# Fused attention and two MoE layers on one core: float32 attention for the first 256 tokens, weight loads eight pieces ahead

## The chip, the cores and the metric

One NeuronCore of a Trainium2 chip runs the whole program in one launch. Its engines are TensorE (PE in the profile, its weight loads PEld), VectorE (DVE), ScalarE (ACT), GpSimd (POOL) and SyncE (SP), which issues nearly all of the DMAs. The metric is the device time of one execution in microseconds, the median over runs.

## The reference

q, k and v are 4 batches x 8 heads x 576 tokens x 64 in float32. Attention is causal by blocks of 64; its output, 2304 tokens of 512, goes through a dense layer with an ELU, and that through a second layer with a skip test and one of eight experts for each token:

```python
scores = scale * np.matmul(q, k.transpose(0, 1, 3, 2))
mask = block_i >= block_j                       # blocks of 64 tokens
attn = np.exp(scores - np.max(scores, axis=-1, keepdims=True))
attn = attn / (np.sum(attn, axis=-1, keepdims=True) + 1e-09)
x = np.matmul(attn, v)                          # -> 2304 x 512
h = x @ w_in                                    # 512 x 2048, float64 weights
g = np.where(h > 0.0, h, np.exp(np.minimum(h, 0.0)) - 1.0)
x = g @ w_out                                   # 2048 x 512
# second layer: x @ w_skip > 0 picks the tokens, argmax(x @ w_gate) the expert,
# out = x + gate * (relu(x @ w1[e]) @ w2[e]) for the picked tokens
```

## The kernel before, in words

**Order.** Every operation is first recorded, not issued (the helper `record`, L306, whose line 320 is the line of nearly all rows in the trace). `order` (L159) then places all of them, engine by engine, by a table of costs (`cost`, L323), by priorities (`rc.base`, where -300 puts the start first) and by the time from which an operation may run (`rc.ready`). Each engine executes its list in that fixed order. A list can therefore stand still behind a row that waits, SP's list of DMAs too.

**Attention** is done for tiles of 128 queries (numbered n = 0 to 4 in a batch) and pairs of heads (p = 0 to 3). `prep_k` (L693), `prep_q` (L706) and `prep_v` (L725) load 128 rows of float32 and split them into a high and a low float16 half: the high half on ScalarE, the low one on VectorE. k and q are then transposed, by a DMA from SP ("kt<-k", "qt<-qq"), or for the first two tiles of batch 0 (`early`, L675) on TensorE through `turn` (L679), whose results ScalarE ("qt<-tp") or VectorE ("kt<-tp") copies out of PSUM. v is scaled by its largest square sum, which `vflat` (L621), `vmax` (L626) and `vscale` (L636) find; vflat loads all of a batch's v, 1152 KB. `s_unit` (L739) makes the scores with two float16 products and a mask ("s<-late"). `x_unit` (L761) takes the row maximum on VectorE ("mx<-s") and the exponential on ScalarE ("e<-s,mx", followed by a read of the accumulated sum). `h_unit` (L792) normalises into the high half ("ehl<-e,su", ScalarE), `l_unit` (L828) makes the low half (VectorE) and transposes the probabilities to et, by DMA or, for the early tiles, by `turn`. `pv` (L848) multiplies by v in three float16 products into PSUM ("xps") and ScalarE copies the result into xt, the input of the first layer.

**First layer.** The tokens go in nine chunks c of 256. w_in and w_out are float64, so each comes as 16 pieces of 512 KB (`raw_load`, L470), and VectorE makes float32 of a piece by one TENSOR_SCALAR and two SCALAR_TENSOR_TENSOR on its integers (`conv`, L495): "twi" for w_in, "two" for w_out. `load_to` (L1292) and `conv_step` (L1296) decide how many pieces are loaded ahead of the conversion. Chunks 0 and 1 multiply in float32: `l1` (L883) makes 256 columns of h for one of eight hidden blocks f (two pieces of w_in each, 8 matmuls of 128x256 per block shown as "h<-xt,twi x8", each recorded in two), `l1a` and `l1b` the ELU, `l2` (L928) the second product ("y<-two,g", eight rows of the trace a block). c0 does all of l1 and then all of l2; its l2 block f needs w_out pieces 2f and 2f+1. Later chunks use float16 halves of the weights, for which ScalarE sums squares ("sq<-twi", "junk<-two") to find a scale. `post` (L948) and `logits` (L986) carry a finished chunk to the second layer.

c0 holds the tokens of tiles 0 and 1 of batch 0; c1 those of tiles 2 and 3, the units i = 4 to 7 of group G1 (a unit is one head of a tile; tile 4 follows). So c1's l1 needs all four head pairs of these.

The driver (L1321 to 1428) begins with the start sequence, which the change rewrites; after it `conv_step` and the further loads are hung on points of the unit list.

Of the kernel before, what the change touches and what calls it, by code (L numbers as in the profile page):

```python
# [9 lines left out]
F32 = mybir.dt.float32  # L10
F16 = mybir.dt.float16
# [345 lines left out]
@with_exitstack  # L357
def tile_kernel(ctx, tc, q, k, v, w_in, w_out, w_skip, w_gate, w1, w2, out):
    nc = tc.nc
# [266 lines left out]
    def vmax(b):  # L626
# [4 lines left out]
        rc.scalar.activation(out=t, in_=t, func=AF.Square, accum_out=col[:, s + b:s + b + 1])  # L631
        if b == 0:

            rc.ready[len(rc.steps) - 1] = 11.5

# [43 lines left out]
    def turn(out, ins, tag, dve=False):  # L679

        t = ps.tile([128, len(ins), 128], F16, tag=tag, bufs=2, name="tp")
        for x, a in enumerate(ins):
            if isinstance(a, tuple):
                for h in range(2):
                    rc.tensor.transpose(out=t[64 * h:64 * h + 64, x, :], in_=a[h], identity=ident16)
            else:
                rc.tensor.transpose(out=t[:, x, :], in_=a, identity=ident16)
        if dve:
            rc.vector.tensor_copy(out, t)
        else:  # L690
            rc.scalar.activation(out=out, in_=t, func=AF.Copy)

    def prep_k(b, n):  # L693
# [6 lines left out]
        rc.vector.scalar_tensor_tensor(out=k1[0:r, :, 1, :], in0=raw[0:r], scalar=0.25, in1=k1[0:r, :, 0, :], op0=ALU.mult, op1=ALU.subtract)  # L700
        if early(b, n):
            turn(KT[b][:, :, n * 128:n * 128 + r], [k1[0:r, h].rearrange("p a d -> p (a d)") for h in range(H)], "y", True)
            return
        rc.sync.dma_start_transpose(out=KT[b][:, :, n * 128:n * 128 + r], in_=k1[0:r].rearrange("p h a d -> p (h a d)"))

    def prep_q(b, n):  # L706
# [7 lines left out]
        rc.vector.scalar_tensor_tensor(out=qq[0:r, 0, :, 1, :], in0=raw[0:r], scalar=0.5, in1=qq[0:r, 0, :, 0, :], op0=ALU.mult, op1=ALU.subtract)  # L714
        if early(b, n):
            turn(t[:, 0], [qq[:, 0, h].rearrange("p a d -> p (a d)") for h in range(H)], "h")
            turn(t[:, 1], [(qq[:, 0, h, 1], qq[:, 0, h, 0]) for h in range(H)], "h")
            QT[b, n] = t
            return
        rc.sync.dma_start_transpose(out=t[:, 0], in_=qq[0:r, 0].rearrange("p h a d -> p (h a d)"))  # L720
# [18 lines left out]
    def s_unit(b, p, i):  # L739
        n = i // 2  # L740
        w = 128 * (n + 1) if n < 4 else S
        parts = [(0, w)] if w <= 512 else [(0, 512), (512, w)]
        qt, kt = QT[b, n], KT[b]
        mx = sm.tile([128, 4], F32, tag="mx", bufs=4, name="mx")
        tl = []
        for m, (a, e_) in enumerate(parts):
            t = ps.tile([128, e_ - a], F32, tag="s", bufs=3, name="s")
            rc.atom()
            for ps_ in range(2):
                if n < 4:  # L750
# [41 lines left out]
    def h_unit(b, p, i):  # L792
# [6 lines left out]
        if n == 1:  # L799
            rc.vector.tensor_tensor(out=su[:, 0:1], in0=su[:, 0:1], in1=su[:, 2:3], op=ALU.add)  # L800
        rc.vector.tensor_scalar(out=su[:, 4:4 + n], in0=su[:, 0:n], scalar1=1e-9, scalar2=2.0 ** -14, op0=ALU.add, op1=ALU.mult)
        rc.vector.reciprocal(out=su[:, 6:6 + n], in_=su[:, 4:4 + n])
        nu[0] += 1
        if b == 0 and i in G[0][0]:

            pool, tag, bufs = mo, "g", GB
        elif HL.get(("wo", 7)) is not None and nu[0] % 3 == 0:
            pool, tag, bufs = wp, "wo7", 1
# [19 lines left out]
    def l_unit(b, p, i):  # L828
# [10 lines left out]
        n, nk = hl.shape[1:3]  # L839
        y = (4, 2)[x] if b == 0 and x < 2 and p % 2 else x  # L840
        et = ET[b, p, x] = ap.tile([128, n, 2 * nk, 128], F16, tag=f"et{y}", bufs=ET_BUFS[y], name="et")
        if b == 0 and i in G[0][0]:
            hf = hl.rearrange("p u n a c -> p (u n a) c")
            turn(et.rearrange("p u n c -> p (u n) c"), [hf[:, y] for y in range(2 * n * nk)], "h", p % 2 == 1)
            return
        rc.sync.dma_start_transpose(out=et.rearrange("p u n c -> p (u n) c"), in_=hl.rearrange("p u n a c -> p (u n a c)"))

    def pv(b, p, g):  # L848
# [16 lines left out]
        while t0 < t1:  # L865
# [4 lines left out]
            if c < 2:  # L870
                rc.scalar.activation(out=xt(c)[:, p, t0 - c * CT:e_ - c * CT], in_=src, func=AF.Copy, scale=st["x0"])
            else:
# [474 lines left out]
    for x in range(6):
# [633 lines left out]
```

## Time and profile before

| what | us |
|---|---|
| three runs | 726.5, 728.25, 731.14; median 728.25 |
| execution that the profile shows | 724.39 |
| its span | 722.6 |
| busy in the span: TensorE, weight loads, VectorE, ScalarE, GpSimd | 671.3, 462.8, 576.3, 514.2, 78.4 |

A stage table gives an engine's busy time in a stretch; a timeline gives one engine's rows in order, with the idle time before a group and what ended it in square brackets. [...] c0's first product begins at 47.54 us, c1's at 129.33.

### The profile page before, as it was taken

What the parts mean: (1) busy time and instruction counts of PE and PEld (TensorE: products, weight loads), DVE (VectorE), ACT (ScalarE), POOL (GpSimd) and SP (SyncE); (2) the same over time, 40 slices, a digit from 0 to 9 for tenths busy, and PEclk for the clock granted to TensorE, in tenths of its full rate; (3) what the DMA queues carried; (4) which work ended last, traced back from release to release, by engine and by line L of the source; (5) the groups of instructions that cost most, each with busy time, mean ns of one, the idle gap of its engine ahead of it and who ended that gap; (6) DMA issues with size and microseconds to landing.
All of it is one profiled execution on the core that took longest, in us unless ns stands there. A gap on an engine that the chain in (4) does not pass through costs nothing. (4 is left out here: it accounts for less than half of the span.)

```text
span 722.6 us, 17731 instructions
## 1 busy us (share of the span) xinstructions
PE 671.3 (93%) x6665; PEld 462.8 (64%) x6665; DVE 576.3 (80%) x1664; ACT 514.2 (71%) x1090; POOL 78.4 (11%) x119
## 2 busy tenths in 40 slices
PE   4679988999999999989999999999999999999994
PEld 3457643875466666647657667667576667777783
DVE  5897999988999999888969945999778654774653
ACT  5977746999986888678758745766366466887782
POOL 2000000001000100100100000000105033423112
PEclk9559999999999999999999999999999999999998
DMA  8699999895796999899538448918165868898731
GB/s 318 175 278 335 287 288 248 174 198 130 142 190 135 171 198 195 147 183 200 111 61 162 91 71 236 347 59 232 32 205 146 226 137 194 230 243 200 248 119 17
DMA packets 211468, 132.96 MB, mean 184 GB/s; under 512 B 176027, under 2 KB 177061, under 8 KB 210848
## 3 DMA queue, kind: packets, MB, share of 16 engines
q1 hardware_dynamic: 206320, 122.80, 69.6%
q0 software_dynamic: 3952, 6.70, 4.4%
q10 hardware_dynamic: 1088, 2.10, 0.8%
q8 instruction: 57, 0.93, 0.5%
q14 instruction: 51, 0.42, 0.2%
HBM read 73.59 MB, written 12.75 MB: 119 GB/s over the span
## 5 line engine op out<-in xcount | busy, mean ns | idle before, releaser
L320 PE MATMUL h<-xt,win 128*128 128x256 f16 x1344 | 158.4, 273 | 1.6 <-DVE n L320 1.0
L320 PE MATMUL y<-wout,g 128*128 128x512 f16 x672 | 155.7, 379 | 0.0
L320 PEld LDWEIGHTS <-win 128*128 128x128 f16 x1344 | 129.0, 98 | 25.0 <-issue 2.8
L320 PEld LDWEIGHTS <-g 128*128 128x128 f16 x672 | 64.2, 98 | 66.5
L320 ACT ACTIVATE e<-s,mx 128x512 f32<-128x512 f32 (+4 forms) x160 | 82.4, 517 | 25.6 <-DVE mx L320 11.0
L320 ACT ACTIVATE ehl<-e,su 128x512 f16<-128x512 f32 (+4 forms) x160 | 80.5, 550 | 23.1 <-DVE su L320 10.3
L320 DVE SCALAR_TENSOR_TENSOR ehl<-e,su,ehl 128x512 f16<-128x512 f32 (+4 forms) x160 | 82.0, 537 | 12.0 <-ACT ehl L320 11.8
L320 DVE TENSOR_REDUCE mx<-s 128x1 f32<-128x512 f32 (+4 forms) x160 | 74.6, 475 | 5.3 <-PE s L320 4.8
L320 PE MATMUL s<-kt,qt 128*128 128x384 f16 (+5 forms) x384 | 69.5, 309 | 8.4 <-ACT e L320 6.4
L320 PE MATMUL xps<-et,vt 128*64 128x128 f16 (+1 forms) x1440 | 49.6, 217 | 12.4 <-DVE xt L320 3.0
L320 PE MATMUL y<-two,g 128*128 128x512 f32 x128 | 59.5, 603 | 1.6 <-DVE two L320 1.6
L320 PE MATMUL h<-xt,twi 128*128 128x256 f32 x256 | 60.7, 390 | 0.3 <-DVE g L320 0.3
L320 PEld LDWEIGHTS <-vt 128*64 128x64 f16 x1440 | 39.9, 113 | 30.8 <-issue 23.5
L320 ACT ACTIVATE el<-h,col 128x512 f32<-128x512 f32 x56 | 38.2, 683 | 24.7 <-PE h L320 23.8
L320 PEld LDWEIGHTS h<-xt,twi 128*128 128x128 f32 x256 | 48.7, 195 | 7.2 <-DVE g L320 0.7
L320 ACT ACTIVATE g<-el,col 128x512 f16<-128x512 f32 x56 | 40.1, 718 | 18.5 <-DVE el L320 18.1
L320 PEld LDWEIGHTS <-p 128*128 128x128 f16 x984 | 46.1, 98 | 7.7 <-PEq L1820 4.1
L320 PEld LDWEIGHTS <-qt 128*128 128x128 f16 (+1 forms) x384 | 28.6, 104 | 26.5 <-issue 10.6
L320 DVE SCALAR_TENSOR_TENSOR g<-el,col,g 128x512 f16<-128x512 f32 x56 | 41.7, 744 | 3.3 <-ACT g L320 3.1
L1521 DVE SCALAR_TENSOR_TENSOR p<-p,n,p 128x1024 f16<-128x1024 f32 x32 | 40.6, 1280 | 3.4 <-ACT p L1520 3.3
L320 DVE SCALAR_TENSOR_TENSOR el<-h,col,el 128x512 f32<-128x512 f32 x56 | 41.7, 745 | 1.3
L320 PEld LDWEIGHTS y<-two,g 128*128 128x128 f32 x128 | 23.0, 189 | 26.4 <-issue 19.3
(234 smaller groups left out, 1129.6 us busy)
## 6 DMA issues: line engine op xcount, KB each, us to landing
p<-in_moe_w_dram SPq DMA_DIRECT2D x45, 512.0 KB, 6.4
rw<-in_moe_w_in_dram SPq DMA_DIRECT2D x16, 512.0 KB, 7.1
rw<-in_moe_w_out_dram SPq DMA_DIRECT2D x16, 512.0 KB, 5.2
pb<-in_moe_w_dram SPq DMA_DIRECT2D x10, 512.0 KB, 4.0
vflat<-in_v_dram SPq DMA_DIRECT2D x4, 1152.0 KB, 8.7
out_dram<-pay SPq DMA_DIRECT2D x18, 256.0 KB, 3.2
pay_d<-pay SPq DMA_DIRECT2D x18, 256.0 KB, 2.6
raw<-in_k_dram SPq DMA_DIRECT2D x16, 256.0 KB, 4.0
```

The costliest lines, as they stand in the source:

```text
L320: rec.call(e, time, lambda: getattr(self.real, op)(*args, **kw), reads, writes, dma)
L1521: rc.call("dve", 1.2, lambda: nc.vector.scalar_tensor_tensor(out=half(1), in0=raw.t, scalar=sc, in1=half(0), op0=ALU.mult, op1=ALU.subtrac ...
```

## The change

The first two tiles of batch 0 are computed in float32. The host adds two inputs, q0 and k0: the first 256 tokens of q and k with d on the partitions, two heads of a pair above each other. Five kinds of step follow from it:

- `load_early` loads them without any split or transposition. q goes into two tiles, in each of which VectorE has set the other head's 64 rows to zero, so that a product over 128 rows gives one head's scores; k is scaled by 0.125 on ScalarE.
- A score tile is one float32 product and the mask, in place of two float16 products and the mask.
- The normalised probabilities stay float32 ("en", ScalarE only; no low half on VectorE), are turned on TensorE in float32, and are multiplied with unscaled v in one float32 product in place of three; xt of c0 is copied with scale 1.
- Later tiles of batch 0 still need the float16 form of the first 256 keys and values: k of tiles 0 and 1 is loaded again and split later, and now transposed by DMA; vmax, vscale and the v split of these tiles move to later slots.
- The pieces of w_in and w_out may be loaded eight ahead of the conversion instead of four (`x - 8`, `x + 9`), eight at the start.

```diff
-        if x - 4 in CONV:
-            rc.steps[-1][4].add(CONV[x - 4])
+        if x - 8 in CONV:
+            rc.steps[-1][4].add(CONV[x - 8])
...
-        t = ps.tile([128, len(ins), 128], F16, tag=tag, bufs=2, name="tp")
+        t = ps.tile([128, len(ins), 128], F32, tag=tag, bufs=2, name="tp")
...
+    def load_early():
+
+        X0["q"] = [ap.tile([128, 2, 4, 128], F32, tag="qt", bufs=3, name="qx") for h in range(2)]
+        X0["k"] = ap.tile([128, 2, 4, 128], F32, tag="ehl", bufs=2, name="kx")
+        for h in range(2):
+            nc.vector.memset(X0["q"][h][64 - 64 * h:128 - 64 * h], 0.0)
+        for n in range(2):
+            rows = slice(64 * n, 64 * n + 64)
+            rc.sync.dma_start(out=X0["q"][n][rows].rearrange("p n a t -> p (n a t)"), in_=q0[rows, :])
+            rc.sync.dma_start(out=X0["k"][:, n].rearrange("p a t -> p (a t)"), in_=k0[:, 512 * n:512 * n + 512])
+        X0["v"] = ap.tile([128, 2, H, D], F32, tag="qt", bufs=3, name="vx")
...
+    def scale_early(n):
+        rc.scalar.activation(out=X0["k"][:, n], in_=X0["k"][:, n], func=AF.Copy, scale=0.125)
...
-        if early(b, n):
-            turn(KT[b][:, :, n * 128:n * 128 + r], [k1[0:r, h].rearrange("p a d -> p (a d)") for h in range(H)], "y", True)
-            return
         rc.sync.dma_start_transpose(out=KT[b][:, :, n * 128:n * 128 + r], in_=k1[0:r].rearrange("p h a d -> p (h a d)"))
...
+            if early(b, n):
+                rc.tensor.matmul(out=t, lhsT=X0["q"][i % 2][:, n, p, :], rhs=X0["k"][:, 0:n + 1, p, :], start=True, stop=False)
+                rc.tensor.matmul(out=t[:, w - 64:w], lhsT=later16[:, 0:128], rhs=later16[:, 128:192], start=False, stop=True)
...
+        if early(b, x):
+            HP[b, p, x] = mo.tile([128, n, nk, 128], F32, tag="g", bufs=GB, name="en")
+            for u in us:
+                rc.scalar.activation(out=HP[b, p, x][:, u % 2].rearrange("p n c -> p (n c)"), in_=UN[b, p, u][0], func=AF.Copy, scale=su[:, 6 + u % 2:7 + u % 2])
+            return
...
+            if early(b, y):
+                for kt in range(y + 1):
+                    for h in range(2):
+                        rc.tensor.matmul(out=x[64 * h:64 * h + 64, c0:c0 + 128], lhsT=X0["v"][:, kt, 2 * p + h, :], rhs=et[:, h, kt, :], start=kt == 0, stop=kt == y)
+                continue
...
-        load_to(min(nraw[0] + 2, x + 5))
+        load_to(min(nraw[0] + 2, x + 9))
...
-    load_raw("k", 0, 0)
-    load_raw("q", 0, 0)
-    load_to(2)
...
-    prep_k(0, 0)
-    prep_q(0, 0)
...
+    load_early()
...
+    scale_early(0)
+    scale_early(1)
     rc.base = 0
-    for x in range(6):
+    load_to(8)
+    vflat(0)
+    addex(0, L("k", 0, 0), L("k", 0, 1))
+    addex(3, P(prep_k, 0, 0), P(prep_k, 0, 1))
+    ex[6][0:0] = [lambda: vmax(0), lambda: vscale(0)]
+    addex(9, P(prep_v, 0, 0), P(prep_v, 0, 1))
     for x in range(6):
```

SP's list at the start of the program, before (rw are the weight pieces, raw rows of q, k or v):

```order
L320 DMA raw<-in_k_dram 128x512
L320 DMA raw<-in_q_dram 128x512
L320 DMA rw<-in_moe_w_in_dram 128x2x512 x2
L320 DMA raw<-in_k_dram 128x512
L320 DMA raw<-in_q_dram 128x512
L320 DMA vflat<-in_v_dram 128x2304
L320 DMA raw<-in_v_dram 128x512 x2
L320 DMA rw<-in_moe_w_in_dram 128x2x512 x2
L320 DMA raw<-in_k_dram 128x512
L320 DMA raw<-in_q_dram 128x512
L320 DMA rw<-in_moe_w_in_dram 128x2x512
```

The same place now, from behind the four loads of q0 and k0:

```order
L320 DMA vx<-in_v_dram 128x512 x2
L320 DMA rw<-in_moe_w_in_dram 128x2x512 x8
L320 DMA vflat<-in_v_dram 128x2304
L320 DMA raw<-in_k_dram 128x512 x3
L320 DMA raw<-in_q_dram 128x512
L320 DMA rw<-in_moe_w_in_dram 128x2x512
L320 DMA raw<-in_v_dram 128x512
L320 DMA rw<-in_moe_w_in_dram 128x2x512
L320 DMA_TRANSPOSE kt<-k_172 128x8x128
L320 DMA_TRANSPOSE qt<-qq 128x8x128
```

Eight pieces of w_in stand ahead of vflat and of the raw loads, where two did; the transposes of k follow later, k_172 being tile 0 of the keys, and the pieces of w_in from the eleventh on stand behind them.

ScalarE's list up to the copy that completes c1's input, before (xt is that input, "win" and "vt" preparations for later work, "pay" the output of chunk 0):

```order
L320 ACTIVATE e_432,su<-s,mx 128x512
L320 ACTIVATE e_433,su<-s,mx 128x64
L320 ACTIVATE ehl<-e_432,su 128x4x128
L320 ACTIVATE ehl<-e_433,su 128x64
L320 ACTIVATE win_517<-twi_188,col 128x1024
L320 ACTIVATE pay<-y 128x512
L320 ACTIVATE e_450,su<-s,mx 128x512
L320 ACTIVATE e_451,su<-s,mx 128x64
L320 ACTIVATE pay<-y 128x512
L320 ACTIVATE xt<-xps,col 128x256
```

The same place now, up to the same copy:

```order
L320 ACTIVATE e_441,su<-s,mx 128x512
L320 ACTIVATE sq,col<-twi_301 128x1024
L320 ACTIVATE ehl<-e_423,su 128x4x128
L320 ACTIVATE sq,col<-twi_304 128x1024
L320 ACTIVATE ehl<-e_424,su 128x64
L320 ACTIVATE e_442,su<-s,mx 128x64
L320 ACTIVATE e_448,su<-s,mx 128x512
L320 ACTIVATE junk,col<-two_308 128x1024
L320 ACTIVATE ehl<-e_441,su 128x4x128
L320 ACTIVATE ehl<-e_442,su 128x64
L320 ACTIVATE e_449,su<-s,mx 128x64
L320 ACTIVATE xt<-xps,col 128x256
```

The sums of squares of the weights ("sq", "junk") and three more pairs of exponentials now stand between the copies of the chunk's output and this copy; before, the squares of w_in stood ahead of the last conversions.

## Rows read from the trace of the kernel before

**Rows 1.** By stage: busy us of each engine, clock, DMA.

```profile
0.00:20.00 20.00, 8.36 (x80) 6.15 (x81) 9.72 (x31) 11.53 (x20) 3.80 (x38) 1.00 0.88 323
20.00:47.50 27.50, 18.86 (x163) 12.89 (x163) 25.93 (x76) 23.71 (x64) 0.35 (x1) 0.50 0.73 197
47.50:81.00 33.50, 32.93 (x165) 27.03 (x165) 29.44 (x60) 24.53 (x46) 0.00 (x0) 0.95 1.08 317
81.00:129.30 48.30, 41.94 (x311) 19.95 (x309) 46.51 (x123) 29.73 (x68) 0.82 (x4) 1.00 1.05 268
129.30:200.00 70.70, 70.70 (x511) 45.73 (x509) 63.12 (x202) 66.62 (x158) 3.35 (x4) 1.00 0.78 160
```

**Rows 2.** TensorE's timeline: start, busy us, group, idle before.

```profile
47.54 8.60 PE L320 MATMUL h<-xt,twi 128*128 128x256 f32 x32
...
65.65 7.07 PE L320 MATMUL h<-xt,twi 128*128 128x256 f32 x32
...
81.09 3.60 PE L320 MATMUL y<-two,g 128*128 128x512 f32 x8
...
117.51 2.84 PE L320 MATMUL y<-two,g 128*128 128x512 f32 x6 [0.80 <-DVE two L320]
...
123.24 3.70 PE L320 MATMUL y<-two,g 128*128 128x512 f32 x8
...
129.33 1.95 PE L320 MATMUL h<-xt,twi 128*128 128x256 f32 x8
...
133.15 0.28 PE L320 MATMUL s<-kt,qt 128*128 128x256 f16 x1
...
133.75 0.66 PE L320 MATMUL xps<-et,vt 128*64 128x64 f16 x30
...
573.35 0.46 PE L320 MATMUL lp<-wgs,x2t 128*128 128x9 f16 x12
```

**Rows 3.** What VectorE waited for, 0 to 129.3: total, times, longest.

```profile
DVE twi L320 <- DMA rw<-in_moe_w_in_dram: 5.4, 5, 2.4
```

**Rows 4.** VectorE's timeline, two places.

```profile
52.41 0.42 DVE L320 TENSOR_SCALAR twi<-rw 128x512 int32<-128x512 int32 x1
...
53.95 0.55 DVE L320 TENSOR_REDUCE mx<-s 128x1 f32<-128x384 f32 x1
...
122.54 0.68 DVE L320 SCALAR_TENSOR_TENSOR two<-rw,two 128x512 int32<-128x512 int32 x1
```

**Rows 5.** ScalarE by form, 0 to 129.3: busy, mean ns, idle before.

```profile
L320 ACT ACTIVATE sq<-twi 128x1024 bf16<-128x1024 f32 x8 | 8.4, 1053 | 1.2 <-DMA kt<-k 1.1
L320 ACT ACTIVATE e<-s,mx 128x512 f32<-128x512 f32 x12 | 8.1, 679 | 4.4 <-DVE mx L320 2.5 <-DVE ehl L320 1.3 <-PE s L320 0.6
L320 ACT ACTIVATION_READ_ACCUMULATOR e<-s,mx 128x1 f32 x39 | 7.7, 196 | 0.0
L320 ACT ACTIVATE ehl<-e,su 128x512 f16<-128x512 f32 x10 | 6.9, 715 | 8.0 <-DVE su L320 4.0 <-DVE mx L320 3.9
...
L320 ACT ACTIVATE qt<-tp 128x1024 f16<-128x1024 f16 x4 | 4.1, 1022 | 3.8 <-PE tp L320 3.8
```

**Rows 6.** ScalarE's timeline.

```profile
83.11 0.67 ACT L320 ACTIVATE e<-s,mx 128x512 f32<-128x512 f32 x1
...
83.78 0.61 ACT L320 ACTIVATE k<-raw 128x512 f16<-128x512 f32 x1
```

**Rows 7.** SP's queue: a transpose's issue.

```profile
30.56 1.36 SPq L320 DMA_TRANSPOSE kt<-k  x1
...
115.66 4.85 SPq L320 DMA_TRANSPOSE et<-ehl  x1
```

**Rows 8.** DMA, 0 to 130: totals, then KB each and us to landing.

```profile
DMA packets 39318, 35.68 MB, mean 274 GB/s; under 512 B 28948, under 2 KB 29204, under 8 KB 38795
...
rw<-in_moe_w_in_dram SPq DMA_DIRECT2D x16, 512.0 KB, 7.1
...
kt<-k SPq DMA_TRANSPOSE x5, 6.3
```

More of the change, by code (lines that the diff above doesn't have):

```diff
@@ L357, in tile_kernel @@
 @with_exitstack
-def tile_kernel(ctx, tc, q, k, v, w_in, w_out, w_skip, w_gate, w1, w2, out):
+def tile_kernel(ctx, tc, q, k, v, w_in, w_out, w_skip, w_gate, w1, w2, q0, k0, out):
     nc = tc.nc
@@ L631, in vmax @@
         rc.scalar.activation(out=t, in_=t, func=AF.Square, accum_out=col[:, s + b:s + b + 1])
-        if b == 0:
-            rc.ready[len(rc.steps) - 1] = 11.5
     def vscale(i):
@@ L679, in turn @@
     def turn(out, ins, tag, dve=False):
-        t = ps.tile([128, len(ins), 128], F16, tag=tag, bufs=2, name="tp")
+        t = ps.tile([128, len(ins), 128], F32, tag=tag, bufs=2, name="tp")
         for x, a in enumerate(ins):
[L683 to L687, printed above, removed]
+            rc.tensor.transpose(out=t[:, x, :], in_=a, identity=ident)
         if dve:
@@ L691, in turn @@
             rc.scalar.activation(out=out, in_=t, func=AF.Copy)
+    X0 = {}
+    def load_early():
[8 more added lines that the diff above has]
+        X0["v"] = ap.tile([128, 2, H, D], F32, tag="qt", bufs=3, name="vx")
+        for n in range(2):
+            rc.sync.dma_start(out=X0["v"][:, n].rearrange("p h d -> p (h d)"), in_=v[0, 128 * n:128 * n + 128].rearrange("p h d -> p (h d)"))
+            RAW["v", 0, n] = X0["v"][:, n]
+    def scale_early(n):
+        rc.scalar.activation(out=X0["k"][:, n], in_=X0["k"][:, n], func=AF.Copy, scale=0.125)
     def prep_k(b, n):
@@ L714, in prep_q @@
         rc.vector.scalar_tensor_tensor(out=qq[0:r, 0, :, 1, :], in0=raw[0:r], scalar=0.5, in1=qq[0:r, 0, :, 0, :], op0=ALU.mult, op1=ALU.subtract)
[L715 to L719, printed above, removed]
         rc.sync.dma_start_transpose(out=t[:, 0], in_=qq[0:r, 0].rearrange("p h a d -> p (h a d)"))
@@ L742, in s_unit @@
         parts = [(0, w)] if w <= 512 else [(0, 512), (512, w)]
-        qt, kt = QT[b, n], KT[b]
+        if not early(b, n):
+            qt, kt = QT[b, n], KT[b]
         mx = sm.tile([128, 4], F32, tag="mx", bufs=4, name="mx")
@@ L800, in h_unit @@
             rc.vector.tensor_tensor(out=su[:, 0:1], in0=su[:, 0:1], in1=su[:, 2:3], op=ALU.add)
-        rc.vector.tensor_scalar(out=su[:, 4:4 + n], in0=su[:, 0:n], scalar1=1e-9, scalar2=2.0 ** -14, op0=ALU.add, op1=ALU.mult)
+        rc.vector.tensor_scalar(out=su[:, 4:4 + n], in0=su[:, 0:n], scalar1=1e-9, scalar2=1.0 if early(b, x) else 2.0 ** -14, op0=ALU.add, op1=ALU.mult)
         rc.vector.reciprocal(out=su[:, 6:6 + n], in_=su[:, 4:4 + n])
+        if early(b, x):
[3 more added lines that the diff above has]
+            return
         nu[0] += 1
-        if b == 0 and i in G[0][0]:
-            pool, tag, bufs = mo, "g", GB
-        elif HL.get(("wo", 7)) is not None and nu[0] % 3 == 0:
+        if HL.get(("wo", 7)) is not None and nu[0] % 3 == 0:
             pool, tag, bufs = wp, "wo7", 1
@@ L833, in l_unit @@
         su = SU.pop((b, p, x))
+        if early(b, x):
+            hl = HP.pop((b, p, x))
+            for u in us:
+                UN.pop((b, p, u))
+            y = (4, 2)[x] if p % 2 else x
+            et = ET[b, p, x] = ap.tile([128, 2, x + 1, 128], F32, tag=f"et{y}", bufs=ET_BUFS[y], name="et")
+            turn(et.rearrange("p u n c -> p (u n) c"), [hl[:, u, c] for u in range(2) for c in range(x + 1)], "h", p % 2 == 1)
+            return
         for u in us:
@@ L839, in l_unit @@
         n, nk = hl.shape[1:3]
-        y = (4, 2)[x] if b == 0 and x < 2 and p % 2 else x
+        y = x
         et = ET[b, p, x] = ap.tile([128, n, 2 * nk, 128], F16, tag=f"et{y}", bufs=ET_BUFS[y], name="et")
[L842 to L845, printed above, removed]
         rc.sync.dma_start_transpose(out=et.rearrange("p u n c -> p (u n) c"), in_=hl.rearrange("p u n a c -> p (u n a c)"))
@@ L870, in pv @@
             if c < 2:
-                rc.scalar.activation(out=xt(c)[:, p, t0 - c * CT:e_ - c * CT], in_=src, func=AF.Copy, scale=st["x0"])
+                rc.scalar.activation(out=xt(c)[:, p, t0 - c * CT:e_ - c * CT], in_=src, func=AF.Copy, scale=st["x0"] if c else 1.0)
             else:
@@ L1968 @@
     arrays, args = {}, []
-    for name in _INS:
-        a = inputs[name]
-        a = _np.ascontiguousarray(a.transpose(0, 2, 1, 3) if name in "qkv" else a)
+    for name in _INS + ['q0', 'k0']:
+        a = inputs[name[0] if name in ('q0', 'k0') else name]
+        if name in ('q0', 'k0'):
+            a = a[0, :, 0:256].reshape(4, 2, 2, 128, 64).transpose(1, 4, 2, 0, 3).reshape(128, 1024)
+        elif name in 'qkv':
+            a = a.transpose(0, 2, 1, 3)
+        a = _np.ascontiguousarray(a)
         if a.dtype == _np.float64:
```

18 lines of the change are left out of this document (2 added, 16 removed).

## The prediction

> **What bounds the kernel now.** I read the stage table first. From 129.3 us on TensorE is busy throughout (70.70 of 70.70 us in the first stretch) and decides; ahead of that it is not: 8.36 of 20, 18.86 of 27.5, 32.93 of 33.5 and 41.94 of 48.3 us [rows 1]. The change touches only work that lies ahead of that point, so the question is when the second token chunk (c1) can start its first product with w_in, 129.33 us now [rows 2]. From there on the two programs issue the same matmuls in the same order, but for what one has already done.
>
> TensorE's own timeline shows three steps up to there [rows 2]: c0's first product (l1) starts at 47.54, its second (l2) at 81.09 with 3.60 us a hidden block, and the last of those eight blocks at 123.24. Inside l2 TensorE waits for converted weights (0.80 us for "two" at 117.51, one of two such waits). The converter is VectorE: the last instruction on w_out starts at 122.54 and ends as the last l2 block starts [rows 4]. So l2 ends when VectorE has converted its 32 pieces and done the attention work that the order puts between. In 20 to 47.5 it is busy 25.93 of 27.5 us, in 81 to 129.3 46.51 of 48.3 [rows 1].
>
> **Part 1, the first 256 tokens in float32 (start of c0's l1).** Removed ahead of 47.5: four qt evacuations of 1.02 us on ScalarE [rows 5] with the k and q splits that they waited for, VectorE's low halves of 16 probability rows and the two kt copies. Added: two VectorE memsets and two ScalarE scalings, small beside these. Up to the last row that c0's l1 needs, the new VectorE order has 8 conversions at 1.54 us a piece (52.41 to 53.95 [rows 4]), or 12.3 us, and 12 us of maxima, sums, copies and memsets: 24 us, where now 35.65 us are busy (9.72 + 25.93 [rows 1]). With 7 us of idleness (10.3 in the first 20 us now) while the first loads land and scores, exponentials and transpositions follow each other, I put the start at 31 us (28 to 36). The gain there is 16 us.
>
> **Part 2, conversion.** An l1 block takes 3.53 us (7.07 for two), at half clock 4.30 [rows 2], so l1 would end near 62 to 63 and ask its last w_in piece near 58. The 16 w_out pieces follow, with the attention units of tiles 2 to 5 and g. Counted in the new order by such steps, VectorE has 84.6 us of work up to its last conversion; the old order has 104.7 and takes 123.2, so it idles 18.5 us. 5.4 us of this is waiting for w_in loads [rows 3], which loading eight ahead should remove at first. But the new SP queue has four kt transposes ahead of w_in pieces 10 to 16, two of them new there, and each waits for VectorE's low half of k. A transpose holds the queue for 1.36 us to 4.85 us [rows 7]. I leave 15 us of idleness in place of 18.5: 99.7. Bounds are 95 (ten idle) and 107.
>
> The loads are the second bound on that. Up to its last w_out load the new queue moves some 28 MB (32 weight pieces, three vflat, 4.3 MB of q, k and v, 3.4 MB of transposes and copies). The profile moved 35.68 MB in its first 130 us at 274 GB/s, the stretch with most w_out loads at 268, the best stretch at 323 [rows 1, 8]. That gives 102, 104 and 87 us for the last landing. Rate and conversion meet, so I take 101 us for the last conversion, 22 us earlier than now. [...]
>
> **Part 3, what stands behind the last conversion.** Now c1's l1 follows the last w_out conversion by 6.1 us (123.2 to 129.33), since the attention of c1's tokens (tiles 4 to 7) ran beside the conversions. In the new ScalarE order much of it comes after: from the row released just ahead of the last two conversions to the last copy into c1's xt stand 13 exponentials (7 of 512 columns), 12 normalisations (7 of 512), one vflat square, six weight squares ("sq", "junk"), and 11 rows of preparing and copying. By durations (0.68 + 0.20 for an exponential of 512 with its read of the sum, 0.72 for a normalisation, 1.05 + 0.20 a square, less for narrower rows [rows 5]) that is 33.2 us. Each of the 63 rows, reads included, overlaps the next by 0.1 us (an exponential of 0.67 at 83.11 and its read of 0.20 have made room for the next row at 83.78 [rows 6]): 26.9 us. It starts about 2.5 us ahead of the last conversion. ScalarE now idles 8.0 us ahead of its normalisations of 512 columns, all for VectorE [rows 5]; without conversions in the way I keep two stalls in the chain, one on copying xt behind the last l2 block and one on the scale of v, 2.4 us each. So c1's l1 starts at 101 - 2.5 + 26.9 + 4.8 = 130.2 us, against 129.33: 0.9 us later. **The 16 and 22 us gained ahead are given back here.**
>
> [...] TensorE has done more by then: 30 attention products (0.66), one set of scores (0.6, from 133.15 to 133.75) and two router products (0.46 each, by the row of such a product later) [rows 2]: -2.2 us. [...]
>
> Sum: +0.9 - 2.2 + 1.5 = +0.2 us on a span of 722.6. The execution profiled took 724.39 us, so it would take 724.6; the median of the three runs before, 728.25, is 3.9 above it, and so is the prediction, **728.5 us**.
>
> **Rivals.**
> (A) Faster: last conversion at 95 and a gap without the two stalls, ScalarE starting on the chain at 92.5: 92.5 + 26.9 = 119.4, -9.9 against 129.33, -2.2, no clock loss: -12.1, 716 us. For it: VectorE is free of conversions in the gap, and 5.4 us of waits for w_in go. Against: the rates of Part 2, and that ScalarE, which shares each unit with VectorE step by step, was busy for only 29.73 of 48.3 us in 81 to 129.3 [rows 1]. Chance 0.28.
> (B) Slower: SP runs in order, so a kt transpose that waits for VectorE holds the w_in pieces behind it. Three blocks of 4.85 us are 14.5; l1 can absorb about 5 of these, as it runs 3.53 us a block while two pieces convert in 3.09. That is 9.5 us at the last conversion: +9.5 + 0.2: 738 us. It decides from the point where the last w_in conversion starts later than about 63 us. Against it: now the same queue holds up VectorE for only 5.4 us. Chance 0.12.
> (C) The loads come no earlier. A piece takes 7.1 us to land at the median and a kt transpose 6.3 [rows 8], and DMA is busy from 47.5 on; at 268 GB/s the last piece lands at 104 to 105 and is converted at 107, 6 later than in my sum: +6.2, 734.5 us. Chance 0.12.
> My forecast has 0.48.
>
> **Numbers.** One per cent, 7.3 us, is what I call a change. Range: from near A, 717, to near B, 737; left out are the outer halves of A and B. Forecast by itself: 722 to 733. Faster by over 1% (below 721): A less its weak half plus the lower tail of the forecast, 0.28. Slower (above 735.5): B, nearly half of C and the forecast's upper tail, 0.22. Within: 0.50.
>
> **What would show it.** c0's l1 at 28 to 36 us; first l2 block near 63; last w_out conversion at 95 to 107, with under 5 us of VectorE waits for w_in; then 25 to 31 us to c1's l1, in which ScalarE is busy nearly throughout and TensorE under half. c1 at 129 to 134, and the remaining 590 us as now. It is wrong if ScalarE's chain in the gap is shorter than 25 us because VectorE let it run beside the conversions, if loads put the last conversion beyond 107, or if the stretch behind c1 changes by over 3 us.

## The result, and the profile after

The changed kernel takes **739.35 us** (median of 732.88, 739.13, 739.56 and 741.07) against 728.17 for the kernel before on the same chip: ratio 1.0136, interval 1.0099 to 1.0173. It is slower; the forecast of no change was wrong, and 739.35 lies above its range. A second set of runs gave 733.66 against 726.28, 1.0118 [1.0081, 1.0154]. The two ratios agree, the two profiles less so: the execution of 739.56 us has a span of 737.8, that of the second set 728.8, against 722.6 before. What both show is the effect of the change; what only the first shows is told apart below.

The stages of the changed kernel, cut where its own steps lie (stretch, length, busy us and instructions of PE, PEld, DVE, ACT and POOL, TensorE's granted clock as a share of full speed, DMA share, GB/s), answer to [rows 1]:

```profile
0.00:20.00 20.00, 12.53 (x68) 8.48 (x68) 11.98 (x45) 11.23 (x36) 3.60 (x37) 1.00 0.93 310
20.00:32.00 12.00, 8.31 (x56) 4.95 (x55) 11.84 (x34) 9.49 (x27) 0.35 (x1) 0.75 0.70 262
32.00:68.70 36.70, 33.77 (x157) 27.83 (x155) 32.12 (x61) 17.70 (x33) 0.00 (x0) 0.90 0.96 249
68.70:106.00 37.30, 34.78 (x147) 15.87 (x145) 33.84 (x73) 24.04 (x46) 0.00 (x0) 1.00 1.06 336
106.00:134.70 28.70, 15.79 (x217) 10.56 (x217) 22.36 (x98) 25.50 (x62) 0.61 (x3) 0.59 1.09 233
134.70:200.00 65.30, 65.30 (x466) 43.90 (x463) 56.50 (x158) 60.20 (x140) 3.62 (x5) 0.97 0.71 149
```

The fifth line is what was not there before: 28.7 us between c0's last l2 block and c1's l1 in which TensorE is busy for 15.79 us, at a mean granted clock of 0.59 (0.50 from 112 to 138 us), and ScalarE for 25.50. TensorE's timeline (start, busy us, group, idle before) gives the steps of [rows 2] now:

```profile
32.02 21.29 PE L320 MATMUL h<-xt,twi 128*128 128x256 f32 x88
53.15 0.33 PE L320 MATMUL s<-kt,qt 128*128 128x384 f16 x1
...
68.71 10.57 PE L320 MATMUL y<-two,g 128*128 128x512 f32 x24
...
102.28 3.70 PE L320 MATMUL y<-two,g 128*128 128x512 f32 x8 [0.20 <-DVE two L320]
...
116.37 1.17 PE L320 MATMUL s<-kt,qt 128*64 128x512 f16 x8 [2.72 <-ACT e L320]
...
129.55 2.45 PE L320 MATMUL xps<-et,vt 128*64 128x128 f16 x42
...
132.83 0.49 PE L320 MATMUL lp<-wgs,x2t 128*128 128x9 f16 x12 [0.45 <-DMA x2t<-pay]
...
133.75 1.01 PE L320 MATMUL xps<-et,vt 128*64 128x64 f16 x30
134.69 5.62 PE L320 MATMUL h<-xt,twi 128*128 128x256 f32 x16
...
141.09 3.62 PE L320 MATMUL h<-xt,twi 128*128 128x256 f32 x16
```

c0's l1 starts at 32.02 (47.54 before), its l2 at 68.71 (81.09), the last l2 block at 102.28 (123.24). All of that gain, 15.5, 12.4 and 21.0 us, is gone at c1's l1: 134.69 against 129.33. Its first block of 16 products takes 5.62 us where the next takes 3.62.

VectorE's waits up to 140 us (total, times, longest) and the end of its conversions answer to [rows 3, 4]:

```profile
DVE two L320 <- DMA rw<-in_moe_w_out_dram: 1.2, 2, 0.8
...
DVE twi L320 <- DMA rw<-in_moe_w_in_dram: 0.4, 1, 0.4
```

```profile
100.35 2.48 DVE L320 SCALAR_TENSOR_TENSOR two<-rw,two 128x512 int32<-128x512 int32 x4
102.75 0.69 DVE L320 SCALAR_TENSOR_TENSOR qq<-raw,qq 128x512 f16<-128x512 f32 x1
```

The loads no longer hold it up (5.4 us for w_in before, 0.4 now). Behind c1 the same instructions stand in both kernels, so one row of each shows how far the end has moved. Here are ScalarE's exponential for the ELU in the first layer of a later chunk, and the last scaled output of the run, in the kernel before, in the changed one, and in its second set:

```profile
361.29 0.69 ACT L320 ACTIVATE el<-h,col 128x512 f32<-128x512 f32 x1 [0.58 <-PE h L320]
...
712.62 0.47 ACT L320 ACTIVATE o<-y,gp 128x256 f32<-128x256 f32 x1 [1.91 <-PE y L320]
```

```profile
371.74 0.69 ACT L320 ACTIVATE el<-h,col 128x512 f32<-128x512 f32 x1 [0.53 <-PE h L320]
...
727.86 0.47 ACT L320 ACTIVATE o<-y,gp 128x256 f32<-128x256 f32 x1 [1.84 <-PE y L320]
```

```profile
367.01 0.69 ACT L320 ACTIVATE el<-h,col 128x512 f32<-128x512 f32 x1 [0.53 <-PE h L320]
...
718.73 0.47 ACT L320 ACTIVATE o<-y,gp 128x256 f32<-128x256 f32 x1 [1.92 <-PE y L320]
```

The first execution is 10.5 us behind at the first place and 15.2 at the second, the other 5.7 and 6.1. c1's l1 is 5.36 us late in the first and 4.76 in the second (134.09). So about 6 us, nearly all of them there by c1's first block, are common to both; the other 9 came later, in one execution, between 143 and 372 us and in the last 150. The four executions of the first set differ by 8.2 us among themselves, so that these 9 need no cause in the change.

### The profile page after: what moved, and what is told of

Read it like the earlier page. It is cut to its first block, busy times and chain, and to the rows that moved or that the text cites. A ratio compares the mean times of both kernels' runs of the same rounds, so it can differ in the third digit from the quotient of the medians.

```text
span 737.8 us, 17507 instructions
## 1 busy us (share of the span) xinstructions
PE 677.5 (92%) x6553; PEld 466.8 (63%) x6553; DVE 575.0 (78%) x1646; ACT 509.4 (69%) x1086; POOL 79.3 (11%) x118
## 4 chain that ended last, share of the span: by engine, by line
DMA 28%; PE 25%; issue 24%; DVE 14%; ACT 3%; SPq 2%; POOL 2%; POOLq 0%; DVEq 0%; ACTq 0%
PE h L320 10%; DMA out_dram<-o,gp 9%; PE y L320 8%; DMA gpa<-pay_d,ah 7%; DMA et<-ehl 4%; PE s L320 3%; DMA lst_d<-li,si 3%; PE xps L320 3%; DVE ehl L320 3%; DVE mx L320 2%; SPq L320 2%; DVE two L320 2%; DMA qt<-qt 2%; DVE twi L320 1%; DVE el L320 1%
## 5 line engine op out<-in xcount | busy, mean ns | idle before, releaser
L320 ACT ACTIVATE ehl<-e,su 128x512 f16<-128x512 f32 (+4 forms) x144 | 74.0, 560 | 15.0 <-DVE su L320 9.0
L320 DVE SCALAR_TENSOR_TENSOR ehl<-e,su,ehl 128x512 f16<-128x512 f32 (+4 forms) x144 | 75.4, 552 | 3.3 <-ACT ehl L320 3.0
L320 PE MATMUL s<-kt,qt 128*128 128x384 f16 (+5 forms) x352 | 63.1, 314 | 11.8 <-ACT e L320 9.9
L320 PE MATMUL h<-xt,twi 128*128 128x256 f32 x256 | 64.6, 409 | 2.9 <-DVE g L320 2.7
L320 PEld LDWEIGHTS h<-xt,twi 128*128 128x128 f32 x256 | 51.4, 206 | 11.8 <-DVE g L320 3.1
L320 PEld LDWEIGHTS <-vt 128*64 128x64 f16 x1368 | 38.1, 115 | 24.2 <-issue 15.8
L320 PE MATMUL xps<-et,vt 128*64 128x128 f16 (+1 forms) x1368 | 46.6, 219 | 7.4 <-DMA et<-ehl 3.9
L320 PEld LDWEIGHTS <-qt 128*128 128x128 f16 (+1 forms) x352 | 26.1, 105 | 32.2 <-issue 18.4
L320 DVE TENSOR_TENSOR hh<-r,hh 128x256 f16<-128x256 f32 x36 | 15.0, 424 | 33.5 <-ACT hh L1676 32.7
```

The source lines that it names most:

```text
L320: rec.call(e, time, lambda: getattr(self.real, op)(*args, **kw), reads, writes, dma)
```

## The experiments

Five theories stood against each other. **Loads**: eight pieces ahead fill the queue and the buffers, and the float32 part alone would be faster. **F**: the float32 part itself costs. **Clock**: the half clock in the gap (granted 0.50 from 112 us on) is the loss. **G**: the conversions stand ahead of c1's attention in the order, so that attention begins late, and ScalarE, which has it all to do then, sets c1's start. **K**: it begins late because the keys of c1 do, behind an SP queue that stands still. For K there were these rows of SP (issue time, us of issue), in the changed kernel:

```profile
20.03 0.38 SPq L320 DMA_DIRECT2D rw<-in_moe_w_in_dram  x1
31.54 1.37 SPq L320 DMA_TRANSPOSE kt<-k  x1
```

From 20.4 to 31.5 us SP issues nothing: the transpose of k waits for VectorE. The first scores of c1's tiles come at 53.15, 10.8 us later than before (42.38), though c0's l1 starts 15.5 us earlier. ScalarE has meanwhile done less. Here is 20 to 81 us, of the changed kernel and of the kernel before:

```profile
20.00:81.00 61.00, 53.23 (x239) 37.68 (x239) 52.91 (x112) 33.23 (x70) 0.35 (x1) 0.89 0.91 270
```

```profile
20.00:81.00 61.00, 51.78 (x327) 39.92 (x327) 55.38 (x136) 48.25 (x109) 0.35 (x1) 0.75 0.92 263
```

33.23 us against 48.25: ScalarE waits through the stretch and works through the gap. The kernel before still has attention of c0 in this stretch, so the count from the start is the fairer one (sums of stage lines): by 81 us ScalarE has been busy for 44.5 us (59.8 before), and from there to c1's l1 for 43.5 (29.7 before).

All ratios here are to the kernel before on the same chip in the same runs. Places such as c1's l1 are read from one execution of each kernel; the two of the changed kernel differ by 0.6 us there.

**e1, four pieces ahead in the changed kernel**

```diff
-        if x - 8 in CONV:
-            rc.steps[-1][4].add(CONV[x - 8])
+        if x - 4 in CONV:
+            rc.steps[-1][4].add(CONV[x - 4])
...
-        load_to(min(nraw[0] + 2, x + 9))
+        load_to(min(nraw[0] + 2, x + 5))
...
-    load_to(8)
+    load_to(4)
```

> The float32 part of the change stays, the weights come four pieces ahead again. Theory G (gap): the early conversions took VectorE ahead of c1's attention, whose chain then stands alone behind the last conversion (28.8 us from y7's end to c1's l1 in the changed kernel) and loses TensorE's clock (0.50 from 111 to 138 us). With four ahead conversions and attention mix again: last w_out conversion near 112 to 118 us, gap under 14 us, clock 1.00 at c1's start, c1's l1 at 124 to 129, time 721 to 727 us. Rival F (the float32 part itself costs, by its two more k transposes and float32 products): c1's l1 stays at 133 or later and the time at 735 or more.

Measured: 1.0132 [1.0089, 1.0176], no better; G's forecast for this run was missed, and F's for c1's l1 (133 or later) came true. Its VectorE waits up to 136 us, the last of them, SP and TensorE:

```profile
DVE two L320 <- DMA rw<-in_moe_w_out_dram: 6.3, 2, 3.9
DVE twi L320 <- DMA rw<-in_moe_w_in_dram: 5.0, 2, 2.9
```

```profile
125.03 0.43 DVE L320 TENSOR_SCALAR two<-rw 128x512 int32<-128x512 int32 x1 [3.89 <-DMA rw<-in_moe_w_out_dram]
```

```profile
14.18 0.47 SPq L320 DMA_DIRECT2D raw<-in_v_dram  x1
26.86 1.36 SPq L320 DMA_TRANSPOSE kt<-k  x1
28.27 0.56 SPq L320 DMA_DIRECT2D rw<-in_moe_w_in_dram  x1
```

```profile
127.50 1.84 PE L320 MATMUL y<-two,g 128*128 128x512 f32 x2 [3.90 <-DVE two L320]
...
130.27 2.43 PE L320 MATMUL y<-two,g 128*128 128x512 f32 x4
...
136.35 3.72 PE L320 MATMUL h<-xt,twi 128*128 128x256 f32 x16
```

VectorE waits 11.3 us for pieces here, as rival B would have it, and SP stands for 12.2 us before a transpose that waits for VectorE. The waits for pieces end late, though, at 62.8 and 71.0 us (w_in) and at 109.0 and 125.0 (w_out); that they go back to SP's silence of 14.7 to 26.9 us no run shows. The last of them holds l2: the last w_out piece is converted 25 us later than in the changed kernel, and c1's l1 stands 3.65 us behind the end of l2 (132.70). So there is hardly a gap, the granted clock is 0.94 from 110 to 140 us and c1's first block takes 3.72 us, yet c1 starts at 136.35. The loss is as large with four ahead, but it comes by another way. The loads theory falls as it was put, since the float32 part alone is not faster; how much eight ahead costs in the changed kernel, this run does not show.

**e2, eight pieces ahead alone, in the kernel before**: the numbers of e1's diff the other way round in the kernel before, whose start stays as it was.

```diff
-        if x - 4 in CONV:
-            rc.steps[-1][4].add(CONV[x - 4])
+        if x - 8 in CONV:
+            rc.steps[-1][4].add(CONV[x - 8])
...
-        load_to(min(nraw[0] + 2, x + 5))
+        load_to(min(nraw[0] + 2, x + 9))
```

> The kernel before with the loads eight ahead alone. Theory G: part of the loss comes back here: the conversions end near 110 to 116 us, a gap of 10 us or more opens to c1's l1 at 128 to 133, time 727 to 735. Rival F: loads are harmless, the 5.4 us of waits for w_in go, c1's l1 at 124 to 127, time 722 to 726.

Measured: 1.0033 [1.0, 1.0065]. Its last conversion starts at 109.80 (122.54 before) and c1's l1 at 128.41 (129.33): conversion 12.7 us earlier buys 0.9. With conversion out of the way c1 hardly moves, so that in the kernel before, too, another wait stands close behind it.

**e3, the gap filled with 36 products that nobody reads**, so that the clock stays up

```diff
+        if c == 0:
+            hd = ps.tile([128, 2, CT], F32, tag="h", bufs=2, name="hd")
+            for x in range(36):
+                rc.atom()
+                rc.tensor.matmul(out=hd[:, 0, :], lhsT=tw("wo", 7)[:, 0:128],
+                                 rhs=GT[0, 7][:, 0:256], start=True, stop=True)
+            rc.atom()
```

> The changed kernel with 36 more float32 products of 128x256 (0.43 us each at full clock, result not used) on TensorE in the gap between c0's last l2 block and c1's l1. It prices the clock. If half clock in the gap and in c1's first block costs what the rows say (5.62 against 3.72 us for that block, 2.45 against 1.3 for 42 attention products), the clock stays at 1.00, c1's l1 comes at 131 to 134 and the time falls by 3 to 5 us to 734 to 736. If the chain on ScalarE alone decides and the clock costs nothing, the time stays at 738 to 741.

Measured: 1.0131 [1.0094, 1.0168]. TensorE, and two stage lines:

```profile
125.80 4.15 PE L320 MATMUL hd<-g,two 128*128 128x256 f32 x18
...
134.66 0.22 PE L320 MATMUL s<-kt,qt 128*128 128x128 f16 x1 [2.37 <-ACT e L320]
...
135.62 5.41 PE L320 MATMUL h<-xt,twi 128*128 128x256 f32 x16
```

```profile
106.00:130.00 24.00, 24.00 (x179) 16.90 (x179) 18.00 (x72) 22.16 (x50) 0.41 (x2) 1.00 1.06 241
...
135.60:141.00 5.40, 5.40 (x24) 4.35 (x19) 4.14 (x10) 3.50 (x9) 0.20 (x1) 0.68 1.09 216
```

The granted clock is 1.00 from 106 to 130 us, the scores ahead of c1's l1 take 0.22 us each (0.29 in the changed kernel's gap, at 0.50), and c1 still starts at 135.62, the last wait being 2.37 us for ScalarE. By itself this does not price the clock, for the fillers have a price too: they stand in TensorE's list among the scores and attention products, and with them TensorE is busy for 24.00 of the 24 us from 106 to 130. That the clock in the gap does not set c1's start is shown by e9 below, where c1 starts 5 us earlier out of a gap at a mean granted clock of 0.61. The first block stayed slow (5.41, at a mean clock of 0.68), so what the clock costs in that block was not separated.

**The changed kernel again**

> The changed kernel once more, unaltered, beside the others of this call, so that they have it on the same chip. Theory G: c1's l1 again at 132 to 136 us after a sparse stretch of about 29 us at half clock, 9 to 15 us over the kernel before. If the loss behind c1 was a chance of the first execution, it comes out under 8 us.

Measured: 1.0118 [1.0081, 1.0154], c1's l1 at 134.09, its first block 5.19; told above.

**e5, the keys of c1's first tiles loaded and prepared first**

```diff
+    load_raw("k", 0, 0)
+    load_raw("k", 0, 1)
     load_to(8)
     vflat(0)
...
+    rc.base = -300
+    prep_k(0, 0)
+    prep_k(0, 1)
+    rc.base = 0
...
-    addex(0, L("k", 0, 0), L("k", 0, 1))
-    addex(3, P(prep_k, 0, 0), P(prep_k, 0, 1))
```

> The changed kernel, but the float16 keys of the first two tiles are loaded ahead of the weights and split with the priority of the start. In the changed kernel SP stands from 20.4 to 31.5 us before the transpose of these keys, which waits for VectorE's low half, and c1's first scores come at 53 us, where the kernel before has them at 42. Theory K (this standing queue makes c1's attention late and so the gap): first c1 scores at 41 to 46, gap shorter by 5 us or more, c1's l1 at 125 to 130, time 728 to 733. Theory G alone (the conversions' place ahead of the attention in VectorE's list decides, not when k and q come): first scores earlier, but c1's l1 within 3 us of 134 and the time within 3 us of the changed kernel's.

Measured: 1.0113 [1.0079, 1.0148]. The first scores come at 48.86 and not at 53.15, c1's l1 at 135.64 and not earlier. K by itself falls as the cause: the first scores come sooner, and c1 does not follow.

**e4 and e11, w_out converted three blocks ahead instead of all at once** (the same kernel twice; the places are e11's)

```diff
-        on_q(0, x, lambda x=x: conv_to(2 * (x + 4)))
-    for x in range(8, 12):
-        on_q(0, x, lambda x=x: conv_to(24 + 2 * (x - 7)))
+        on_q(0, x, lambda x=x: conv_to(2 * (x + 4) if x < 8 - 4 else max(16, 16 + 2 * (x - 8 + 3))))
+    for x in range(8, 16):
+        on_q(0, x, lambda x=x: conv_to(min(32, 16 + 2 * (x - 7 + 3))))
```

> The changed kernel (eight ahead), but each w_out piece is listed for conversion three hidden blocks ahead of its use instead of four or more, so that c1's attention comes earlier in VectorE's list. Theory G: last conversion 2 to 5 us later than 102.8, gap shorter by more, c1's l1 at 128 to 132, time 730 to 737. Rival F: no difference, 738 to 741.

> e4 once more, since its first profile shows nothing of an ordinary execution. Theory G: last w_out conversion at 103 to 107, c1's l1 at 130 to 132, time 728 to 730 where the kernel before takes 726.

Measured: 1.0059 [1.0037, 1.008] and 1.0063 [1.0036, 1.0091]; c1's l1 at 129.97 in e11. About half of the loss goes when attention is listed earlier among the conversions, though the last conversion then ends 2.6 us later (its row starts at 102.95).

**e6, without the 16 sums of squares of the weights on ScalarE.** What is left out: constants stand in for the sums, so the scales of the 16-bit weight halves are not those of the data.

```diff
-        sq = ap.tile([128, 1024], BF16, tag="k1", bufs=1, name="sq")
-        rc.scalar.activation(out=sq, in_=tw("wi", j), func=AF.Square, accum_out=col[...])
+        rc.gpsimd.memset(col[...], 2.0)
...
-        junk = ap.tile([128, 1024], BF16, tag="k1", bufs=1, name="junk")
-        rc.scalar.activation(out=junk, in_=tw("wo", j), func=AF.Square, accum_out=col[...])
+        rc.gpsimd.memset(col[...], 0.5)
```

> The changed kernel without ScalarE's 16 sums of squares of w_in and w_out (constants take their place, so the scales of the weights' float16 halves are not those of the data); six of them stand in the gap, 1.15 us each. It prices ScalarE's chain. If that chain sets c1's start: c1's l1 5 to 8 us earlier (127 to 130) and the time 5 to 9 us lower. If the chain waits for VectorE, x2t or transposes instead, c1's l1 moves by under 3 us.

Measured: 1.0029 [0.9999, 1.0058]. TensorE:

```profile
129.94 3.35 PE L320 MATMUL h<-xt,twi 128*128 128x256 f32 x8
```

c1's l1 comes 4.2 us earlier than in the changed kernel of the same runs (134.09). Only 1.5 of this is the copy that completes xt (129.81 against 131.34). The rest is the order: 30 attention products, a set of scores and a router product stand ahead of c1's l1 in the changed kernel and behind it here. In the gap of the changed kernel stand these squares (ScalarE by form, 106 to 134.7; busy us, mean ns, idle before):

```profile
L320 ACT ACTIVATE sq<-twi 128x1024 bf16<-128x1024 f32 x5 | 5.2, 1041 | 0.0
...
L320 ACT ACTIVATE junk<-two 128x1024 bf16<-128x1024 f32 x2 | 2.1, 1048 | 0.0
```

Six of these seven squares lie ahead of the copy that completes xt (the second junk starts at 132.76), 6.3 us of busy time at 1.05 each. Taking all squares away moved the copy by a quarter of that and c1's l1 by two thirds. What ScalarE does in the gap is thus a part of what sets c1's start, and another wait stands close behind it: here TensorE waits 0.99 us for transposed probabilities ahead of the last products for c1 (128.28).

**e9, the squares of w_in asked seven units earlier, and kept**

```diff
-        on_q(0, j + 8, lambda j=j: sq_win(j))
+        on_q(0, j + 1, lambda j=j: sq_win(j))
```

> The changed kernel with that move of the squares alone. e6, without them, gave c1's l1 at 129.94 and 5 us less than the changed kernel. Moved, not removed: c1's l1 at 129 to 131, time 4 to 6 us under the changed kernel (728 to 730), if only their place cost. If they now delay c0's l1 or c1's keys (they share a buffer with the k split), the gain is under 2 us.

Measured: 1.004 [1.0018, 1.0062], c1's l1 at 129.19. The stage line of its gap:

```profile
106.00:129.20 23.20, 14.44 (x174) 9.36 (x172) 20.02 (x85) 20.35 (x49) 0.41 (x2) 0.61 1.08 218
```

Five of the eight squares leave the gap for 69 to 79 us, where ScalarE had idle time, and c1 comes back to its old place at a granted clock about as low as in the changed kernel (0.61 against 0.59); the time stays 0.4% above the kernel before. The copy that completes xt starts at 128.82, 2.5 and 3.2 us earlier than in the two executions of the changed kernel. This is the clearest support for G's second half. It is no proof for ScalarE alone: as in e6, the 30 products and what goes with them stand behind c1's l1 here. And the chain of work followed back from c1's l1 in the trace of the changed kernel has its longest pieces in DMAs, two landings of transposed probabilities and one of x2t, for which the router product ahead of c1's l1 waits (start, us):

```profile
111.55 6.01 DMA et<-ehl
...
121.98 4.42 DMA et<-ehl
...
129.43 3.36 DMA x2t<-pay
```

No run took these away.

**e7, the key loads first and e4's conversions; e8, that and e9's squares**

```diff
+    load_raw("k", 0, 0)
+    load_raw("k", 0, 1)
-    addex(0, L("k", 0, 0), L("k", 0, 1))
... and the lines of e4; in e8 those of e9 too
```

> Early loads of the float16 keys of the first two tiles (their split at its place in the unit list, unlike e5) together with the conversion of w_out listed three hidden blocks ahead (as e4). Theory G: e4's gain stays, 6 to 10 us under the changed kernel, about level with the kernel before (724 to 730); with theory K true as well, 2 to 5 us better still, below the kernel before. If both are wrong it stays within 3 us of the changed kernel.

> e7 with the squares of w_in listed from the first hidden block of c0's l1 on, where ScalarE is idle (33 of 61 us busy from 20 to 81 us in the changed kernel), so that they leave the gap. Theory G with ScalarE's chain as the setter: c1's l1 3 to 6 us earlier than in e7 (130.97), at 125 to 128, time 2 to 5 us under the kernel before (721 to 724 where that takes 726). If VectorE or the transposes have taken over the chain in e7: c1's l1 within 2 us of e7's and the time level with the kernel before.

Measured: 1.0003 [0.9976, 1.0031] and 1.0011 [0.9991, 1.0032]; c1's l1 at 130.97 and 128.61. The loss is gone, but the gain that e8 was expected to bring does not appear. In e8 TensorE's largest wait from 105 to 345 us (2.3 us in the kernel before), and ScalarE's from 85 to 135, are for the transposes of probabilities by DMA:

```profile
PE xps L320 <- DMA et<-ehl: 9.9, 9, 1.8
```

```profile
ACT ehl L320 <- DMA et<-ehl: 4.6, 4, 2.5
```

**e10, the kernel before with the three edits to the order (e2, e4, e9) and no float32 part**: the lines of those diffs.

> The kernel before (no float32 part) with the three moves of e8's lists that it can have: loads eight ahead, w_out converted three blocks ahead, squares early. It asks whether the float32 part is worth anything once the lists fit. Theory G: its VectorE has 8 us more to do ahead of c0's l1, so c1's l1 comes 2 to 4 us later than in e8, time 725 to 728. If the float32 part is worth nothing, it is level with e8 within 2 us.

Measured: 1.0012 [0.9989, 1.0034], c1's l1 at 128.60, as in e8 with the float32 part, and not 2 to 4 us later. With the order mended on both sides, the float32 attention is worth nothing here, in either direction, and F falls as a cost that stays whatever the order. No kernel tried is faster than the kernel before.

All the kernels by c1's start (the first TensorE row of that l1). Where (x4) or (x2) stands, the row is a group of four or two, which takes 2.5 or 1.4 us:

| kernel | last w_out row starts, us | copy that completes xt starts, us | c1's l1, us | ratio |
|---|---|---|---|---|
| before | 122.54 | 127.95 | 129.33 | 1 |
| e2 loads alone | 109.80 | 128.52 | 128.41 | 1.0033 |
| e10 before, order edits | 112.88 | 128.27 | 128.60 | 1.0012 |
| e8 all three | 104.11 | 128.24 | 128.61 | 1.0011 |
| e9 squares early | 100.89 (x4) | 128.82 | 129.19 | 1.004 |
| e6 no squares | 101.87 (x4) | 129.81 | 129.94 | 1.0029 |
| e11 convert later | 102.95 (x4) | 129.50 | 129.97 | 1.0063 |
| e7 keys, convert later | 104.47 | 130.41 | 130.97 | 1.0003 |
| changed, second set | 99.31 (x4) | 131.34 | 134.09 | 1.0118 |
| changed | 100.35 (x4) | 132.05 | 134.69 | 1.0136 |
| e3 fill | 101.57 (x4) | 134.52 | 135.62 | 1.0131 |
| e5 keys early | 102.47 (x2) | 134.19 | 135.64 | 1.0113 |
| e1 four ahead | 126.76 | 135.86 | 136.35 | 1.0132 |

Every kernel with c1's l1 at 131 or earlier is within 0.63% of before, every one with it at 134 or later is 1.13 to 1.36% slower. When the last conversion starts says nothing: it spans 27 us without a relation to the ratio, though in e1 TensorE waits 3.90 us for it. Within the first group c1's start does not order the ratios either (e7 against e11, e9 against the kernel before).

## Why the prediction was wrong

What held:

- **Part 1.** c0's l1 at 32.02, forecast 31 (28 to 36).
- **Part 2.** The conversions end at 102.8, forecast 101; VectorE idles 16.2 of the first 106 us (89.78 busy, the sum of four stage lines), forecast 15 up to 99.7. Waits for w_in fall to 0.4. Loads did not bind: 1.2 us of waits for w_out, at 336 GB/s in 68.7 to 106, above every stretch that I had [rows 1], and at 388 in a part of it (the line below). The rates of 268 to 323 that I went by were too low. l2 began at 68.7 and not at 62 to 63, which cost nothing, since its last block still waited 0.20 us for the last conversion.

```profile
73.80:92.20 18.40, 16.86 (x54) 7.50 (x53) 15.31 (x34) 9.01 (x16) 0.00 (x0) 1.00 1.04 388
```

- **Part 3, the gap.** ScalarE's chain from 101.50 to the end of the xt copy at 132.5 is 31.0 us, forecast 26.9 + 4.8 = 31.7. That it came so near is luck in part: ScalarE is busy for 27.96 us of it and idle for 3.1, so that one term was too small and the other too large. The two rows at its ends, and the stretch between:

```profile
101.50 0.61 ACT L320 ACTIVATE qq<-raw 128x512 f16<-128x512 f32 x1
...
132.05 0.47 ACT L320 ACTIVATE xt<-xps,col 128x256 f32<-128x256 f32 x1 [0.43 <-PE xps L320]
```

```profile
101.50:132.52 31.02, 18.22 (x188) 10.80 (x182) 24.90 (x97) 27.96 (x65) 0.61 (x3) 0.66 1.08 236
```

What failed, all in Part 3 and its sum, which put c1's l1 at 130.2 (it came at 134.69) and took 2.2 us off behind it:

- **"It starts about 2.5 us ahead of the last conversion."** The chain starts 1.3 us ahead of 102.8. With the 1.8 us by which the conversion itself came late, that is +3.0 at c1's start; the shorter chain gives 0.7 back.
- **"-2.2 us" for attention and router products that TensorE has done by then.** This credit had the wrong sign: what is done by then can be done because it stands ahead of c1's l1. The sum also let c1 start where ScalarE's chain ends; in the kernel before, c1's l1 follows the end of the copy (128.42) by 0.9 us, with 30 attention products between (the two rows below). In the changed kernel it follows by 2.2 (132.5 to 134.69), at a granted clock of 0.50: TensorE waits for x2t, then come a router product, a set of scores and 30 attention products (1.01 in place of 0.66). Thirty such products stand ahead of c1's l1 in both kernels, so they were no credit at all. Nor did the time that the others would have saved behind c1's l1 show: at VectorE's first g of c1 the lag is 6.9 us (142.83 against 135.96). Start and this: 130.2 + 3.0 - 0.7 + 2.2 = 134.7.

```profile
127.95 0.47 ACT L320 ACTIVATE xt<-xps,col 128x256 f32<-128x256 f32 x1 [0.37 <-PE xps L320]
```

```profile
128.47 0.66 PE L320 MATMUL xps<-et,vt 128*64 128x64 f16 x30
```

- **"+1.5" for the clock.** These 1.5 us are the 8.60 less the 7.07 of [rows 2], two blocks each, the first two right behind the stretch that [rows 1] gives at 0.50; that c1 would lose as much was my estimate, and no run shows the term by itself. What the runs showed in its place: c1's first block took 5.62 us, at a mean granted clock of 0.65 (134.69 to 140.31), against 3.62 for the next, and 1.5 of the difference shows at g. So the place was right, and so nearly was the size. The granted clock is 0.59 over the sparse stage, 0.50 from 112 to 138 us, with TensorE busy for 15.26 of these 26 us, and 1.00 from 140.3 on. The blocks of 4.30 that Part 2 puts at half clock ran at a mean of 0.82 (47.54 to 56.14 before).
- **"The remaining 590 us as now."** In the second set it held (4.8 us late at c1, 6.1 at the end), in the first not (5.4 and 15.2). I have no cause for that difference; the instructions are the same.

So the sum should have been +5.4 at c1 and +6 to +7 at the end. The second set's profile has that (6.2 us of span), the medians lie 7.4 and 11.2 us over those of before.

Underneath the sums lies one misreading. I hung the chain on the last conversion and took the rows in it, and their order, as given. The experiments show that, with the conversions early, c1's start depends on when attention for its tiles comes up in the order and on how much of ScalarE's work is left for the end: 12.7 us of earlier conversion bought 0.9 in e2, conversions listed later took back about half of the loss in e11, and five squares listed ahead of the gap gave back 5 us at c1's l1 in e9, 2.5 to 3.2 of them at the copy. How much of the rest lies with the landing of transposes is open. Rival A failed on this too: it had ScalarE begin at 92.5. Rival B had a time near the measured one (738) for a reason that did not act: VectorE waited 0.4 us for w_in. In e1 VectorE did wait 5.0 us for w_in. The 5 us that l1 was to absorb are 3.5 by the prediction's own figures, eight blocks of 0.44. C fell with the 1.2 us of waits.

Left open: why the stretch behind 143 us cost 9 us more in one execution than in another. Further, why e7 is better than e4 and e11 (1.0003 against 1.0059 and 1.0063, the intervals apart) with c1 no earlier than in e11, when early keys by themselves (e5) did nothing. And e7 prepares the keys at another place than e5, so the two are not a clean pair.

## What to carry to other kernels

Work that is made earlier brings the end no nearer unless the work behind it moves with it: before pricing a gain of 16 or 22 us, list what each engine still has to do between the step that gains and the step that decides, and see whether an engine that idles now will be the one that is needed then. Sums of squares and similar side work belong where their engine idles, which an earlier first stage may have shifted. Instructions "already done" are a credit only if they do not stand ahead of the step whose start is being forecast. And an edit to one engine's order moves rows on the others: compare the last input of the deciding step as well as its start.

## What the runs showed of the hardware

- SP issued nothing while a DMA transpose in its list waited for VectorE, with plain loads behind it: 11.1 us of silence in the changed kernel (20.4 to 31.5, the next weight pieces at 34.95), 12.2 in e1 (14.7 to 26.9, the next weight piece at 28.27). VectorE's waits for w_in came to 0.4 us with eight pieces ahead and to 5.0 with four; how much of that the silence caused was not separated.
- With the gap filled with products the granted clock was 1.00 from 106 to 130 us (e3), where the changed kernel has 0.50 from 112 to 138, and c1's first block, behind a last wait of 2.37 us, ran at a mean of 0.68 and was slow all the same (5.41 against 3.62).
- In the changed kernel the DMA moved 336 GB/s over 37 us of weight loads and transposes (68.7 to 106), and 388 over 18 us within them (73.8 to 92.2).
